# Six gate operations of each batch move from VectorE to GpSimd, and the listed order is laid out anew

## The chip, the cores and the metric

The kernel runs on one core of one Trainium2 chip, as one launch. The metric is device time in microseconds (us), the lower the better. Before the change the median of three runs was 641.9 us (641.13 to 643.39).

## The reference

The program computes an attention layer with a decay and feeds its result into a mixture of experts, each of which is an attention layer of its own. There are 8 batches, 8 heads, 576 positions, a head dimension of 64, 4 experts, and two experts are chosen for each position.

```python
# attention with decay, for each batch and head
scores = scale * np.matmul(q, k.transpose(0, 1, 3, 2))
log_f = np.log(np.clip(f, 0.0001, 1.0))
cum = np.cumsum(log_f, axis=-1)
decay = cum[:, :, :, None] - cum[:, :, None, :]
scores = np.where(causal, -1000000000.0, scores + decay)
scores = scores - np.max(scores, axis=-1, keepdims=True)
attn = np.exp(scores)
attn = attn / (np.sum(attn, axis=-1, keepdims=True) + 1e-09)
attn_out = np.matmul(attn, v)
# x = attn_out with the heads side by side: (batch, position, 512)
logits = x @ w_gate
topk = np.argpartition(-logits, K, axis=-1)[..., :K]          # K = 2
w = softmax of the two chosen logits
for e in range(E):                                            # 4 experts
    q, k, v = x @ wq[e], x @ wk[e], x @ wv[e]
    ye = causal_softmax(scale * q @ k.T) @ v @ wo[e]
    out += (e is chosen) * w * ye
```

## The kernel before, in words

**Units of work.** The kernel works on pairs: two heads of one batch (32 units of kind `a`), or two experts of one batch (16 units of kind `m`). Each unit goes through `max_pass` (the row maxima of the scores, found with one cheaper product), `scores` (the scores again, more exactly, as two products that accumulate in PSUM, then the exponential) and `attend` (the product with the values). Two units form a group, for which `row_sums` and `apply_rows` divide by the sums of the exponentials. For a batch's experts `moe_front` first makes the values and the gate logits (`pv`, line 439), then the gates; `prep_moe` makes queries and keys (`pp`, line 544); `project_out` multiplies by the output weights (`po`, line 936).

**Engines.** TensorE makes all products. VectorE takes the maxima out of PSUM with a masked reduction (line 624, with an accumulator that is read by a second instruction, and line 640), and makes the low parts of numbers that are split in two (lines 399, 557 and 913), the multiplication by the reciprocal sums (line 886) and small steps. ScalarE makes the exponentials (lines 734, 744, 750, 765) and copies out of PSUM. GpSimd cuts the causal diagonals out of the exponentials (line 703), and adds the exponentials of a unit up to a narrower tile, `R`, in four additions (lines 776, 778, 780, 782), whose columns TensorE then sums (line 839).

**The gates** (lines 469 to 525, in `moe_front`). With `lg` the logits of 128 positions by 5 blocks by 4 experts, `g4` and `t4` (128 by 80 numbers) hold for each pair of experts whether one is at least as large, and larger, than the other. `g4` is multiplied by an upper triangle (477), `t4` by a lower one (479), and the two are added (481), so that a tie goes to the lower number. `wins` counts and compares with 1.5 (484, 486). Then `mx` is the largest logit (489), `gt` the difference (492), its exponential on ScalarE (494), its product with `wins` (496), `sm` its sum, plus 1e-9, and the reciprocal (499, 501, 503), and `gt` times that (505). TensorE turns the gates with 16 small products (`pg`, line 512), VectorE copies them to `gc` (521, 525), and `row_sums` of the experts multiplies the reciprocal sums by `gc` (862).

**Order.** Each task (one of the functions above for one unit, group or batch) is a Python generator; each `yield` ends a step. `ORDER` is a text of 4939 steps: two characters name the task whose next step is issued. At the end every instruction is tied to the one before it on its engine, so each engine runs its own instructions in the order of this text, and the five engines and the DMA queue of SyncE (SP) meet only where one waits for another's data or buffer:

```python
    for x, y in zip(digits[::2], digits[1::2]):
        i = DIGITS.index(x) * len(DIGITS) + DIGITS.index(y)
        ...
        next(started[i], None)
    ...
        if ins.engine in behind:
            tc.add_manual_dep(ins, behind[ins.engine], order, reason="in order")
```

`SLOTS` lists in the same way which buffer each new tile takes: the 8 banks of PSUM, 20 strips, 5 wide tiles and so on. The 110 matrix products of `keep_warm` (`warm`, line 205) do no work for the result; 100 of them stand in the list before the first product of `scores`.

**The start and the end.** The first unit has a maximum pass of its own form (`max_by_head`, lines 566 to 606). The last tasks of the list are the `row_sums`, `apply_rows` and `project_out` of the last batch's experts.

Of the kernel before, what the change touches and what calls it, by code (L numbers as in the profile page):

```python
# [32 lines left out]
0e0e0e0e4z0e080303080h080e0e0e080808080h08080808080h08080h0e080e0e0j0j0j0o0t040e0j0j0j0e0e080808080808084w4w080e
0j0j0o0o0j0j0j0j0j0j0j0j0j0j0j0j0j0j0j0j0e0j0o0h0f0f0f0f0o0f0f0o0o0q0f09080j0t0j090f0f080f0f0f0f03080q0A0q0f0q0q
0q0j0j0q0f0f0f0f0q0q0t0q0k0k0k0A0q0k0q0d0f0f0q0k0t0k0k0k0a0t0t0k0a0a0a0a0f0q0F040k0k0k0q0k0q0k0f0k0q0q0f0k0q0i0k
0k0q0q4A0q0q0q0k0k0k0k0k0f0q0v0v0v0v0v0v0f0v0v0v0v0p0v0A0k0q0A0a0A0F0a0g0v0v0v0v0v0v4A0v0v0g0t0k0q0o0v0l0v0q0l0a
0q0q0B0t4y0a090C0C0v0v0v0v0v0C0g0C0C0C0C0C0C0C0C0r0r0r0r0r0r0r0r0b0f0r0r0r0r0r0C0C0C0r0v0v0v0v0C0C0C0r0r0r0r0C0C
0N0C0r0k0r0r0C0C0r0C0C0m0m0m0C0F0F0F0C0m0s0b0m0l4A0O0b0b0m0m0b0b0C0b0C0b0w0w0w0w0w0A0w0w0w0w0w0w0w0w0b0H0H0H0H0H
0H0H0m0m0w0H0N4A0C0C0n0n0H0s0s0N0H0H0n0w0M0w0w0w0w0w0M0n0R0R0n0R0n0n0n0w0w0H0H0H4A0n0R0M0w0w0N0H0H0H0n0H0H0H0H0H
0r0n0H0H0b0A0M0H0N0N0R0R0A0Y0N0N0N0N0u0M0N0N0N0N0N0N0N0N0N0N0N0N0N0N0N0N0N0N0N0N0N0N0N0O0N0D0M0D0R0D0D0O0O0O0D0N  # L40
0r0O0O0r0O0M0M0O0O0D0D0D0D0O0D0N0H0D0D0O0O0D0D0O0D0D0D0O0O0G0F0O0O0O0D0H0H0O0w0r0w0D0H0F0F0x0H0N0D0D0D0Y0x0O4y0y
0b0+0y0M4A0I0Y0Y0Y0Y0I0I0I0O0O0N0O0M0M0O0I0I0I0I0O0I0I0I0I0I0I0I0I0I0y0I0I0I0I0I0I0I0y0y0y0R0Y0O0O0O0O0R0R0R0R0R
# [40 lines left out]
322X31312X31302T2X2X2T2X2T2T2X2X2X322T30302T2X3132303032322T303030302T2T2T2B2T3032313230302C303030302T2C302T3232
2T2X2T3c312X3c2X302I302C2C302C31312N2O2C322T2N2I322O2T2T322X2I323e32323232322Y323c2Y2O32322Y2Y2Y2Y2T2T2T2Y2O2Y35
3c2Y2Y32324y3e323e352Y2Y2Y2Y2Y3e322Y2Y2O2O3e3e2Y2Y2Y2Y2Y2Y2Y32323c2C4y3235353c353535353535352Y353535352Y35353535
35353535353535353532353h2T3e3e353e3e35352O2N3e332O2U35353o352C2C303333332C30303e3e333e2U3c36363636363636362U2D36
# [957 lines left out]
```

## Time and profile before

| | |
|---|---|
| Median of three runs | 641.9 us (641.13 to 643.39) |
| The profiled execution's own time | 642.41 us |
| Its span, from the first to the last instruction | 640.7 us |
| TensorE (PE) busy | 627.2 us, 98% |
| VectorE (DVE) busy | 541.1 us, 84% |
| ScalarE (ACT) busy | 481.9 us, 75% |
| GpSimd (POOL) busy | 409.7 us, 64% |
| DMA queue of SP, share of 16 engines | 43.7% |

A busy TensorE is not a TensorE at its peak: the products are pipelined, their ends are modelled, and idle times under 150 ns count as busy. So the 2% that are left are stalls that can be told one by one, with the engine that ended each. An instruction of VectorE or GpSimd is shown from its start to its end, which holds whatever kept it from its data.

### The profile page before, as it was taken

To read this page: it belongs to the slowest core of one execution; us is meant where nothing else is said; L and a number is where in the kernel's file an instruction comes from. 1 tells how busy PE (TensorE), PEld (TensorE's weight loads), DVE (VectorE), ACT (ScalarE), POOL (GpSimd) and SP (SyncE) were. 2 spreads that over 40 slices of the span, in tenths; PEclk is the share of its full clock that TensorE was granted. 3 is DMA by queue.
4 is the path that set the end of the run, shared out by engine and by line. 5 is a ranking of instruction groups with operands and counts; after the bars stand their busy time and mean duration, and the time that the engine had idled before them with its cause. 6 is when DMAs were issued, how large, how long until landed. Compare 5 with 4: busy or idle time off the path is not lost.

```text
span 640.7 us, 15170 instructions
## 1 busy us (share of the span) xinstructions
PE 627.2 (98%) x5303; PEld 538.1 (84%) x5303; DVE 541.1 (84%) x1541; ACT 481.9 (75%) x1057; POOL 409.7 (64%) x519
## 2 busy tenths in 40 slices
PE   8899999999999999989999999999999999999997
PEld 6677889789888988869888898887987789879976
DVE  6889998898988988988998898889788987787572
ACT  7899887897778867867688877877667896566654
POOL 8999499638748585284569664655848647533740
PEclk9999999999999999999999999999999999999999
DMA  6556425533555355512552461552435433241425
GB/s 195 154 168 194 136 55 143 137 90 96 141 140 130 80 158 144 161 55 62 170 145 66 148 174 40 139 142 83 119 105 136 134 109 76 79 98 21 107 70 202
DMA packets 33531, 76.90 MB, mean 120 GB/s; under 512 B 4395, under 2 KB 4875, under 8 KB 33455
## 3 DMA queue, kind: packets, MB, share of 16 engines
q1 hardware_dynamic: 33455, 75.94, 43.7%
q8 instruction: 42, 0.69, 0.4%
q14 instruction: 34, 0.28, 0.1%
HBM read 32.86 MB, written 10.35 MB: 67 GB/s over the span
## 4 chain that ended last, share of the span: by engine, by line
PE 88%; DVE 6%; issue 2%; DMA 2%; ACT 1%; SPq 1%; POOL 0%; DVEq 0%; POOLq 0%
PE pp_m L544 16%; PE ob_a L801 10%; PE pv L439 7%; PE po L936 7%; PE s_a L716 7%; PE s_a L717 7%; PE m_a L618 6%; PE m_m L618 4%; PE ob_m L801 4%; PE oa_a L801 4%; PE s_m L716 4%; PE s_m L717 4%; PE sm_a L839 3%; PE warm L205 2%; PE oa_m L801 1%
## 5 line engine op out<-in xcount | busy, mean ns | idle before, releaser
L703 POOL TENSOR_SCALAR_AFFINE_SELECT P_a<-P_a 128x256 f32<-128x256 f32 x128 | 65.3, 527 | 112.7 <-ACT P_a L734 67.2
L716 PE MATMUL s_a<-ka_a 128*128 128x320 f32 (+4 forms) x384 | 104.2, 296 | 1.1 <-DVE mxs_a L624 0.9
L717 PE MATMUL s_a<-kq 128*128 128x320 f32 (+4 forms) x384 | 102.9, 294 | 0.0
L624 DVE CUSTOM_DVE_ANT_0 junk_a<-m_a,mask 128x192 bf16<-128x192 f32 (+2 forms) x186 | 86.8, 486 | 17.3 <-PE m_a L618 15.4
L618 PE MATMUL m_a<-kq 128*128 128x448 f32 (+3 forms) x372 | 80.7, 304 | 4.0 <-DVE mxs_a L624 3.1
L552 ACT ACTIVATE kq<-pp_m 64x288 fp32r<-64x288 f32 x128 | 51.9, 406 | 31.6 <-PE pp_m L544 30.1
L716 PEld LDWEIGHTS s_a<-ka_a 128*128 128x128 f32 (+1 forms) x384 | 69.2, 180 | 4.4 <-DVE mxs_a L624 1.6
L717 PEld LDWEIGHTS s_a<-kq 128*128 128x128 f32 (+1 forms) x384 | 68.6, 180 | 1.2
L557 DVE TENSOR_TENSOR ka_m<-pp_m,kq 64x288 fp32r<-64x288 f32 x128 | 58.2, 454 | 12.9 <-ACT kq L552 9.7
L801 PE MATMUL ob_a<-P_a,va 128*64 128x320 f32 (+1 forms) x512 | 67.5, 406 | 0.0
L776 POOL TENSOR_TENSOR R_a<-P_a 128x896 f32<-128x896 f32 x32 | 67.5, 2110 | 0.1
L618 PEld LDWEIGHTS m_a<-kq 128*128 128x128 f32 (+1 forms) x372 | 57.6, 180 | 9.7 <-DVE mxs_a L624 4.4
L703 POOL TENSOR_SCALAR_AFFINE_SELECT P_m<-P_m 128x256 f32<-128x256 f32 x64 | 33.7, 543 | 48.2 <-ACT P_m L734 31.0
L778 POOL TENSOR_TENSOR R_a<-R_a,P_a 128x640 f32<-128x640 f32 x32 | 55.3, 1731 | 1.8
L801 PEld LDWEIGHTS ob_a<-P_a,va 128*64 128x64 f32 x512 | 35.8, 137 | 24.0
L716 PE MATMUL s_m<-ka_m 128*128 128x192 f32 (+2 forms) x192 | 51.8, 295 | 0.0
L717 PE MATMUL s_m<-kq 128*128 128x192 f32 (+2 forms) x192 | 50.9, 294 | 0.0
L624 DVE CUSTOM_DVE_ANT_0 junk_m<-m_m,mask 128x192 bf16<-128x192 f32 (+2 forms) x96 | 44.9, 485 | 5.3 <-PE m_m L618 4.3
L399 DVE TENSOR_TENSOR ka_a<-xin_a,ka_a 64x1152 fp32r<-64x1152 f32 x32 | 47.9, 1497 | 0.7
L734 ACT ACTIVATE P_a<-s_a 128x512 f32<-128x512 f32 x64 | 36.8, 598 | 13.2 <-PE s_a L717 12.0
L399 DVE TENSOR_TENSOR ka_a<-xin_a,kq 64x1152 fp32r<-64x1152 f32 x29 | 42.5, 1465 | 0.8
L618 PE MATMUL m_m<-kq 128*128 128x320 f32 (+3 forms) x192 | 41.2, 298 | 0.0
(204 smaller groups left out, 2025.3 us busy)
## 6 DMA issues: line engine op xcount, KB each, us to landing
xin_a<-in_qk_dram SPq DMA_DIRECT2D x32, 576.0 KB
va<-in_v_dram SPq DMA_DIRECT2D x32, 320.0 KB
bt_a<-rr_a SPq DMA_DIRECT2D x32, 288.0 KB
ka_m<-kq SPq DMA_DIRECT2D x32, 288.0 KB
kq<-ka_a SPq DMA_DIRECT2D x30, 288.0 KB
out_dram<-outb SPq DMA_DIRECT2D x32, 256.0 KB
...
```

The lines of the kernel that those rows point to most:

```text
L399: eng.tensor_tensor(lo, x[at], hi.bitcast(F32), ALU.subtract)
L544: nc.tensor.matmul(pp[:, :HS], w[:, c, es], x[c][:, gs], start=(n == 0), stop=(n == 3 * KC - 1))
L552: nc.scalar.activation(hv[h], src[h], AF.Copy)
L557: nc.vector.tensor_tensor(lo[:, h, gs], src[h], hv[h].bitcast(F32), ALU.subtract)
L618: nc.tensor.matmul(dst, qB[0:K, h, i0 : i0 + dst.shape[0]], kB[0:K, h, j0:j1], start=True, stop=True)
L624: nc.vector.tensor_tensor_reduce(jk[:, :n], src, mask[:, MW - n :], 1.0, init, ALU.add, ALU.max, acc)
L703: return nc.gpsimd.affine_select(pv, pv, [[0, 2], [1, 128]], ALU.is_ge, 0.0, base=0, channel_multiplier=-1)
L716: nc.tensor.matmul(dst, kaf[:, c : c + m], qA[:, h, i0:i1], start=True, stop=False)
L717: nc.tensor.matmul(dst, kqf[0:K, c + h * S : c + h * S + m], qB[0:K, h, i0:i1], start=False, stop=True)
L776: g.tensor_tensor(r[:, :, 128:S], p[:, :, 320:768], p[:, :, 768:1216], ALU.add)
L778: g.tensor_tensor(r[:, :, 256:S], r[:, :, 256:S], p[:, :, 1216:1536], ALU.add)
L801: mm = nc.tensor.matmul(dst[64 * h : 64 * h + 64, c0 : c0 + rhs.shape[-1]], vs[h][0:kp, blk], rhs, start=first, stop=last,)
```

## The change

Six operations of the gates are issued on GpSimd and no longer on VectorE: the two products with the triangles and their addition, the subtraction of the largest logit, the product with `wins`, and the product with the reciprocal. The steps and their number stay what they were: the same 4939 steps stand in the new list, in another order, and the slots are dealt out anew. No other instruction is added or taken away. In the new list 107 of the 110 `warm` products stand before the first product of `scores`.

```diff
 ORDER = """
-4w4w4w4w4w4w4w4w4w4w4w4w4w4x4x4x4w4w4y4w4w00024w004w4w004x074y014x0005054A4A054w4w4w4w4w4w4w4w4w4w4w4w4w4w4w4w4w
-4w4w4w4w4w4w4w4w4w4w4w4w4w4w4w4w4w4w4w4w4w4w4w4w4w4w4w4w4w4w05024y4y4y4y4w4y4y4w4w4w4y4w4w4w4A4A4A4A4A4A4A4A4A4A
...
+4w4w4w4w4w4w4w4w4w4w4w4w4w4w4w4w4w4w4w4w4w4w4w4w4w4w4w4w4w4w4w4w4w4w4w4w4w4w4w4w4w4w4w4w4w4w4w4w4w4w4w4w4w4w4w4w
+4w4w4w4x4x4x4x00020507004x004y4y4y4y004y4y4y4y4A4A4A4A4x4A4A4A4A4A4w4w4w4w4w4w4w4A4w4w05054A4w4A4w024w4w4w4w4w4w
...
 SLOTS = """
-P 01201201201021021021012010210120120120102101201021
+P 01201201201021020120102101201021012012010012010120
...
         nc.vector.tensor_tensor(t4, la, lb, ALU.is_gt)
         yield
-        nc.vector.tensor_tensor(g4, g4, up.unsqueeze(1).to_broadcast([128, 5, E, E]), ALU.mult)
-        yield
-        nc.vector.tensor_tensor(t4, t4, low.unsqueeze(1).to_broadcast([128, 5, E, E]), ALU.mult)
-        yield
-        nc.vector.tensor_tensor(g4, g4, t4, ALU.add)
-        yield
+        nc.gpsimd.tensor_tensor(g4, g4, up.unsqueeze(1).to_broadcast([128, 5, E, E]), ALU.mult)
+        yield
+        nc.gpsimd.tensor_tensor(t4, t4, low.unsqueeze(1).to_broadcast([128, 5, E, E]), ALU.mult)
+        yield
+        nc.gpsimd.tensor_tensor(g4, g4, t4, ALU.add)
+        yield
...
         gt = work.tile([128, 5, E], F32, tag="gt", name=f"gt{b}")
-        nc.vector.tensor_tensor(gt, lg, mx.unsqueeze(2).to_broadcast([128, 5, E]), ALU.subtract)
+        nc.gpsimd.tensor_tensor(gt, lg, mx.unsqueeze(2).to_broadcast([128, 5, E]), ALU.subtract)
         yield
         nc.scalar.activation(gt, gt, AF.Exp)
         yield
-        nc.vector.tensor_tensor(gt, gt, wins, ALU.mult)
+        nc.gpsimd.tensor_tensor(gt, gt, wins, ALU.mult)
         yield
...
-        nc.vector.tensor_tensor(gt, gt, sm.unsqueeze(2).to_broadcast([128, 5, E]), ALU.mult)
+        nc.gpsimd.tensor_tensor(gt, gt, sm.unsqueeze(2).to_broadcast([128, 5, E]), ALU.mult)
         yield
```

## Rows read from the trace of the kernel before

**Rows 1.** The page: span, busy time by engine, TensorE in 40 slices

```profile
span 640.7 us, 15170 instructions
...
PE 627.2 (98%) x5303; PEld 538.1 (84%) x5303; DVE 541.1 (84%) x1541; ACT 481.9 (75%) x1057; POOL 409.7 (64%) x519
...
PE   8899999999999999989999999999999999999997
```

**Rows 2.** Busy time by stretch: length, then PE, PEld, DVE, ACT, POOL

```profile
0.00:48.00 48.00, 41.71 (x308) 33.21 (x309) 38.55 (x106) 40.27 (x62) 45.09 (x56) 1.00 0.56 172
48.00:273.00 225.00, 225.00 (x1935) 193.89 (x1935) 202.97 (x583) 181.35 (x399) 151.83 (x197) 1.00 0.49 129
273.00:284.00 11.00, 8.65 (x71) 6.58 (x65) 9.89 (x20) 7.61 (x17) 9.87 (x10) 1.00 0.22 60
284.00:429.00 145.00, 145.00 (x1275) 126.29 (x1274) 127.10 (x375) 109.36 (x243) 88.14 (x113) 1.00 0.43 115
429.00:437.00 8.00, 7.60 (x60) 5.99 (x58) 7.31 (x15) 7.18 (x16) 7.80 (x11) 1.00 0.72 208
437.00:622.00 185.00, 184.21 (x1599) 160.09 (x1601) 149.67 (x436) 126.86 (x303) 106.95 (x137) 1.00 0.35 92
622.00:640.70 18.70, 15.03 (x73) 12.10 (x69) 5.63 (x12) 9.24 (x21) 0.00 (x0) 0.99 0.57 186
```

**Rows 3.** Waits of TensorE's products: us in total, times, longest

```profile
PE m_a L618 <- DVE mxs_a L624: 3.1, 4, 1.1
...
PE mp_a L685 <- DVE mxs_a L624: 1.3, 2, 0.7
...
PE s_a L716 <- DVE mxs_a L624: 0.9, 1, 0.9
```

**Rows 4.** VectorE in order of time, 273 to 284 us and at 430: start, duration

```profile
274.57 2.54 DVE L913 TENSOR_TENSOR xl_a<-ot_a,xh_a 128x576 fp32r<-128x576 f32 x1
...
280.53 2.15 DVE L913 TENSOR_TENSOR xl_a<-ot_a,xh_a 128x576 fp32r<-128x576 f32 x1
...
430.15 3.83 DVE L886 TENSOR_TENSOR ot_a<-bt_a,ot_a 128x576 f32<-128x576 f32 x2 [0.47 <-DMA bt_a<-rr_a]
```

**Rows 5.** GpSimd in order of time, 273 to 284 us

```profile
274.39 2.10 POOL L776 TENSOR_TENSOR R_m<-P_m 128x896 f32<-128x896 f32 x1
...
279.96 2.11 POOL L776 TENSOR_TENSOR R_m<-P_m 128x896 f32<-128x896 f32 x1
```

**Rows 6.** TensorE's products in order of time, 273 to 284 us

```profile
280.66 0.39 PE L618 MATMUL m_a<-kq 128*128 128x256 f32 x1 [1.06 <-DVE mxs_a L624]
...
283.42 1.03 PE L618 MATMUL m_a<-kq 128*128 128x448 f32 x6 [1.14 <-DVE mxs_a L624]
```

**Rows 7.** Groups by line, the six operations: busy us, mean ns, idle before

```profile
L505 DVE TENSOR_TENSOR gt<-gt,sm 128x20 f32<-128x20 f32 x8 | 3.2, 398 | 0.2
...
L496 DVE TENSOR_TENSOR gt<-gt,wins 128x20 f32<-128x20 f32 x8 | 2.7, 333 | 0.8 <-ACT gt L494 0.8
...
L492 DVE TENSOR_TENSOR gt<-vm,mx 128x20 f32<-128x20 f32 x8 | 2.3, 287 | 0.2
...
L481 DVE TENSOR_TENSOR g<-g,t 128x80 f32<-128x80 f32 x8 | 2.2, 274 | 0.2
...
L477 DVE TENSOR_TENSOR g<-g,up 128x80 f32<-128x80 f32 x8 | 2.0, 247 | 0.0
...
L479 DVE TENSOR_TENSOR t<-t,low 128x80 f32<-128x80 f32 x8 | 1.8, 225 | 0.0
```

**Rows 8.** Lines 913, 782 and 614: duration ns, min/median/max, first and last start

```profile
L913 DVE TENSOR_TENSOR xl_a<-ot_a,xh_a x32: 694/754/2540, 67.3 to 576.1; 128x576 fp32r<-128x576 f32 x32
...
L782 POOL TENSOR_TENSOR R_a<-R_a,pl x32: 447/454/1652, 47.3 to 563.5; 64x128 f32<-64x128 f32 x32
...
L614 POOL MEMSET mxs_a<- x31: 92/95/102, 5.4 to 527.1; 64x2 f32 x31
```

**Rows 9.** Chain that ended last, its end: start, duration

```profile
622.53 14.52 PE po L936 x63
```

More of the change, by code (lines that the diff above doesn't have):

```diff
@@ L33 @@
[L33 to L42, printed above, removed]
@@ L83 @@
[L83 to L86, printed above, removed]
-2O3e333333333e3333362D362D35333333332T36353636363636363e3e3e3333362W36332D333333333336303e3e3e3e3h3h3h36363e3636
@@ new lines @@
+4w4w4w4w4w4w4w4w4w054A0505004A4A00004w0005020202020202020202020c4w4w4w4w4w4w024y4y4y4z024w4w4w014w02020602020202
+0702020707024w4w074z0c074w024w4w4w4w4w4w4w0202020202024w0c000c07020202070707070c050c0303070c07070707070707074w07
+0h4w03030303034z4z4z07070303030303030e0e0e07030303070e0e0e0303030e4w0307074z4z4z07030e0303070d0e0e0j0e0e0e0e0h0e
+0e0e0h0504040c070c0h0h040e0e0e0808030308080808080h0h0e0e0e08080808080e0e08080e080j0j0j0j0j0j080e08030e080o0j0j0j
+0j08080j0j0o0j0t08080j0o0j0j080j0j0j0j0q0j0j0j0j0j0h0e0e0f0f0f0f0f0f0f0f0f0f0f08080f0o0o0o0o0j090j0f0t0f0f0f0f08
@@ new lines @@
+090q0q0q0f0q0q0q0q0q0q0j0j0t0k0f0k0k0k0k0k0k0k0f0f0A0q0t0t0k0k0k0k0k0t0i0q0q0q0q0q0q0q0q0q0q0q0q0f0a0f0a0a0k0k0k
+0k0k0p0v0k0q0v0k0q0v0a0v0v0f0v0k0A4A0F0A0a0A0a0v0v090v0v0g0k0g0v0f0a0k0v4A0g0v0v0v0v0v0v0v0v0v0v0q0v0q0A0k0q0q0o
+0q0k0k0t0l0a0C0C0C0t0l0F0v0f0v0a0v0C0C0C0C0C0C0C0l0r0r0r0r0r0r0r0r0r0r0r0r0v0C0v0r0b0C0b0r0C0v0C0r0C0C0C0C0r0C0v
+0r0r0C0C0m0F4A0r0w0m0r0r0r0m0m0m0b0m0b0w0w0w0w0w0w0w0w0F0C0F0m0b0b0w0b0b0w0w0w0C0C0s0m0A0C0b0m0s0w0s4A0H0H0H0H0H
+0w0w0w0H0w0H0n0H4y0H0n0n4A0M0N0N0N0w0H0R0R0R0n0n0n0n0n0H0w0M0M0n0n0N0R0w0H0H0C0H0H0H0H0H0H0H0C0M0H0A0H0N0N0M0N0N
@@ new lines @@
+0N0N0N0N0C0R0w0H0O0N0N0N0N0w0C0N0N0C0w0A0N0N0N0N0N0N0N0N0N0N0N0N0N0N0N0N0M0N0H0D0D0M0M0Y0M0u0H0O0O0O0O0B0H0r0r0D
+0D0H0O0M0H0D0D0O0w0O0M0D0w0D0O0r0O0D0D0D0D0D0r0D0D0D0D0H0O0O0F0O0O0O0O0O0O0O0O0H0D0D0D0D0R0F0F0O0O0x0y0y0n0y0y0y
+0Y0Y0M0N0O0O0I0I0I4A0G0I0I0I0I0I0O0I0I0I0I0N0I0N0I0I0I0I0I0x4A0Y0Y0Y0O0O0O0I0O0I0I0Y0R0R0R0S0R0b0M0R0R0R0R0R0R0R
+0R0R0R0R0R0R0R0+0x0D0+0+0+0+0+0I4y0R0R0R0+0R0R0R0R0D0P0b0R0R0R0+0+0+0M0M0I0y0+0S0S0S0S0M0M0M0S0S0S0S0P0I0I0P0S0S
+0M0M0O0P0P0y0P0M0+0S0S0S0S0S0P0P0P0P0P0P0P0S0+0P0R0D0M0S0M0S0D0D0P0+0P0P0S0S0S0P0P0P0P0P0S180S0S0S0+0+0Y0+0+0+0+
@@ new lines @@
+0+0+0R0+110I0y0R0z0M180M0R0M0M0M0M0M0M0M0y0P0+0S0S0S0M0S0P0J0E110K110E0+0z0+0+0+0T0K0M0M0J0M0P0J0E0M0T0T0T0T0T0T
+0T0M0z0z0T0T0T130K0P1111111313131313131313131f110T0+0+130T0T0T0T0T0T0T180T0T0Q0-18180K0K0Q0M0T0T1313130Z0M131313
+0K13130-1d0-0Q0-13131313130M0T0-120-0-0-0-0-130-0-0-0-0-0-0-0K0-0-13130K0K1a1a1a0M0z0z0z0z1a1a1a1a1a1a1a0T1a0M0M
+0-0-0-131813110L0M1d1d0M180U0U10100U130L1a141a0L141a141a1a1414141414141414141k14141d1d0T0L14141014190L0z0L0L1a1a
+1a1a0z0L1l1l1a1a1a1a1a1l0L1f1a141414140V0M1a1e0V0V1l0-141a1a0M0M1f181a1f1f1f1l1l1f1l1f1l1w0V1f0V0V1l1l1p1l1f1l1l
@@ new lines @@
+1l1b1l1l1b1l1b1b1l1l1l1l1l1l1b1b1b1k1k1k1k1k1b1b1f1f1d0-0V0V1b1b1f1f1f1f1f1f1f1f1f0-4A4A1b4A4A0V1l1l1l1l1l1l1l1l
+1l1p1f1b1b1k1k1k1k1b1l1l1f1f1m1f1p1d1d1b141k1b0z1f1m1b14141l1l141f1f1p1p1p1p1f0W1p1p0-1m1p1p1p1m1m1m1b1b1b1b1m1f
+1p1m1m1b1p1p1p1p1p1p1p1l1l1b0W0L1q1p1p1p1p1p1p1p1p1p1p1p1p1p1p1q161b1q1q1q161w160L1q1g1g1g1g1g1g1q1q161g1q1q1B16
+1g1g1g1g161m1k1q0V1m161g1k1k1k1g1g1g1g1g1g1g1g1g160W1b1m1m1m1m1g1g1k1k1g1g1k0W1q1q1q1q1m1m1m1g1m1m1m1m1m1q1q1q1m
+1q1w1q1q1q1q1w171B1m1c1m171w151h1w0W1h151m1k1m1m1y1y1p1m1k1p151w0W0W1y1p0W1y1k1k1k1k1y1y1y1y0W1y1c1c1I1k1k1k1n1n
@@ new lines @@
+1k1n1k1k1q1q1n1n1n1n1n1y1n1n1n1p1q1n1q1k1k1k1n1n1n1q1y1n1n1n1D1i1i171i1i1q1q4A1h1y1y1y1y1y1y1y1y1y1y1y0X1n1n1n1B
+1I1n1n1k1k171r1B1B17161r1r1r1r1r1r1r1r1r1r1r1r1C1r1r1r1y1B1n1y1r1r1N1n1y1y1B1r1r1r1o1o1o1I1I1I1B1y1D1i1D1D1D1D1r
+1r1r1D1D1D0X0X1D1r1y0X0X0X1D1x1D1D1D1i1D1D1D1y1D1D1D1s1s1n171D171y0X171k1i1s1D1w0X1D1i1i1J1N1K1K1K1K1K1K1K1K1K1K
+1D0X0X1D1D1z1z1K1r1z1z1z1z1z1z1z1K171k1K0X1z1K1K1K1K1k1k1k1k1z1K1z1K1K1K1D1D0X1D1D1z1z1z1j1k1k0X0X1k1K1j1z1z1z0X
+1j1k1k1t1k1t1U1K1K1z1N1N1N1V1V1k1k1z1j1j1j1j1V1V1j1j1E1N1E1E1E1E1E1E1U1U1E1K1K1E1E1E241E1E1P1t1U1E1E1E1E1E1E1E1E
@@ new lines @@
+1E1I1I1K1K1V1V1V1V1V1V1Z1P1P1Z1K1V1P1P1P1P1P1P1P1P1V1V1K1E1I1U1V1V1V1W1z1V1Z1Z1Z1L1L1L1L1L1L1Z1U1N1U1U1U1Z1t1L1V
+1P1P1P1L1L1L1L1L1L1L1L1L1L1t1L1Z1t1P1z1P1P1t1t171P171V1V1V1V1V1V1V1V1t1t1L1U1U291z1z1P1V1Z1V1V1V1V0W1Z1W1z1z1P1P
+1V1L1Z1Z1Z1V1W1V1V1V1L0W1V1V1W1W1W1Z1Z1E1E1W1W1W1W1N1E1P1P1P1P1P4y1Z1Z1Z1L1L1Z1Z1Z1Z1Z1Z1Z1Z1Z1Z1Z1Z1Z1Z1P1P1u1G
+1Z1Z1u2g1L1u1u1u1G1F1P1P1L1L1A1A1+1Q1F1F1Q1Q1W1+1Z1Z1+1Z1+1U1+1G1Q1+1+1+1+1A1Q1Q1G1Q1Q1Q1Q1Q1Q1+1Q1G1W1+1W1W1Q1Q
+1W1u1W1W1j1W1W1Q1Q1Q1W1Q1j1W1W1Q1Q1W1W1+1+1+1+1+1Q1Q1G29241W1U1U1U1U1U1U1U1Z1U241O1+1Q1Q1Q1W1G1G1G241U1+1+1+1+1+
@@ new lines @@
+241+1W1W1u1+1+1M1M1M241R1S241u1H1S1S1S1u1u1u1+1S1W1H1H1+1H1+1U1U1U1U1U1U1W1U1U1U1U1U1X1X1X1X1R1R2626261X1X1X1H1H
+1H1v1v1+1X26261v1v1+1U1U26261X2626261S1S1S1U1v1X1X1X1X1X1X261v1X1X1-1X261X2626261X2929291S1X1X1U2626261-1-1-1-1-
+26262626261X1-1-1H26262625291v1v1v1T1-1-1-1v2b1-2a1-1-1-1v1v1v1v1-1-1v291H1v2b1-1-1-261-1v1v2b2b2b2b1v2b2b2b2b1-
+2626261-1-1-1Y2b1U2g2g24202g2b201U1Y1U1T201U1T1T2l1T1T1T2b2b27271U2b2b2b272b2b272b1T1U1U1T1Y272727271U1U1X272b2b
+2s2727272727272i2g2i2i2i2i2i2i2i27272i2i2i2s2s2s2s2s292b2s2b2b2s1v2s2i1-1X2i2i2i2i2b2i2i2i1U2i272i1X2l212i212121
@@ new lines @@
+2g211U2b1U1U2i272b2b2b212s2s2s2s2s2s2s2s2s274y2l212l2s272n2t2t2t2c2c2c2t1H2c2c2c2c2c2c2c2c2c2c2l2l2l2c2c2c4y2i27
+2i2t2i21211H2c2c2c2c2c2c2727272g2t2t2i2t2t2t2t2t2t2t2t2t2t2t2t2t2t2t2c2i2i2i2g2l2n2t2n2n2n2n2n2n2n2t2x2n2t2n2s2s
+2s2s2s2s2s2t2t2t2t2t2t1T2c2n2s2n2n2t2t2c2n2n2n2n1T2n2c2u2t2t2t2j2t2u2n2n2n2j222u2u2u2n2n2s2s2s2n2s2s2s2s2j2u2221
+222822222d222d2n2n2d2u222u282u2j2u2E222s2u2s222n2j2j2j2j2j2j2j2j2n2n272j2j2j2u2s2u2j2j2h282u2u2u2u2u2u2u2u2j2E2u
+2E2u2E2e2e2o2o2o2j2m2j2e2j2j2u2u2x2x2o2o2o2o2o2o2o2o2o2x2x2x2o2o2o2o2o2o2o2o2o2s2x2u2t2e2E2E2Q2e2y2o2o2o2E2o2u2j
@@ new lines @@
+2u2u2x2x2x2x2x2x2x2x2x2x2x2x2x2x2x2x2x2x2x2x2x2x2x2x2x2x2x2x2s2x2x2x2u2e2e2e2J2y2k2y2G2G2y2y2y2y2y2y2G2G2E2y2G2y
+2v2p2p2p2f2k2o2y2y2y2y2v2v2j2f2j2y2y2y2y2v2s2j2y2y2y2v2G2v2v2v2v2v2v2v2v2y2y2f2G2v2s2G2G2y2v2v2G2v2v2v2v2v2G2y2e
+2q2k2q2J2y2v2v2v2G2v2G2G2G2G2G2G2G2G2G2G2G2G2y2G2y2y2G2w2J1v2G2Q2G2s2z2z2z2z2f2z2z2z2z2z2f2z2z2L2w2s2J2J2J232z23
+2f2q2z2f2z2z2z2z2J2v2G2L2z2V232z2z2q2z2q2z2L2L2z2z2z2z2G2L2L2L2L2L2L2L2s2s2q2Q2H2H2323232q2q2q2L2L232L2L2L2L2s2L
+232L232H2J2Q232H232L2H2H2H2H2L2L2L2S2L2Q2f2L2H2H2H2H2H2H2H2H2H2H2H2L2L2L2L2L2H2w2H2r312f2B2s2B2B2A2r2s2s2A2r2r2r
@@ L116 @@
+4i4i4u3L4i4u4u4u4u3L4u3L3L3L3L3L3L3L3L3L4u4u4u4u4u3L3L4j4j4j4j4j4j4j4j4j4j3L3L4j4j4j4j4j4j4v4i4v4v4v4v4v4v4v4v4v
 4v4v4v4v4v4v4v4v4v4v4v
```

117 lines of the change are left out of this document (41 added, 76 removed).

## The prediction

> **What bounds the kernel now.** I read the page first. TensorE is busy for 627.2 of 640.7 us; VectorE comes next with 541.1, and GpSimd has 640.7 - 409.7 = 231 us without work [rows 1]. So the end is set by TensorE, and only its 13.5 us of idle time can be won as long as the products themselves stay what they are; the change touches none of them. Second I asked for busy time by stretch, cut where the 40 slices show less than nine tenths, to see in which stage these 13.5 us lie [rows 2]. The start, up to 48 us, holds 48.00 - 41.71 = 6.3; the end, from 622 us, holds 18.70 - 15.03 = 3.7, which is the way of the last outputs behind the last product; between them lie only 2.35 at 273 to 284, 0.40 at 429 to 437 and 0.79 just behind it, 3.5 together. From 48 to 273 and from 284 to 429 us TensorE has no gap that the profile shows. Third, the waits by engine: what ends the gaps of TensorE is nearly always a maximum that VectorE still owes. The three rows make 3.1 + 1.3 + 0.9 = 5.3 us, those of the start included [rows 3].
>
> Fourth, the two long gaps in order of time, because they show the mechanism on which I build. TensorE stood for 1.06 and for 1.14 us before a product of the maximum pass, which waited for a PSUM bank that VectorE had not yet read [rows 6]. VectorE was late because a subtraction of two tiles in SBUF took 2.54 and 2.15 us [rows 4], while the same instruction has a median of 754 ns and a minimum of 694 [rows 8]. Both began 0.2 and 0.6 us after one of GpSimd's long additions had begun (274.39 for 2.10 us, 279.96 for 2.11 us), and both ended 0.6 us after its end, about what they take alone [rows 4, 5]. The gaps from 429 us on have the same mark ahead of them: two multiplications of two tiles in SBUF took 3.83 us together [rows 4]. So a VectorE instruction with two inputs in SBUF can lose 1.4 to 1.8 us beside an addition on GpSimd, and everything behind it on VectorE's queue is late by as much. This is what the middle of the run still loses.
>
> The Trainium skill names the same thing (GPSIMD Engine Reference, section Specifications): GpSimd's interface to SBUF is shared with VectorE, with contention when a VectorE instruction has two SBUF inputs. By that rule the trace agrees, with 2540 ns against 694 for one instruction [rows 8], and it speaks against a change that puts more two-input work on GpSimd; what it would do here is the third rival.
>
> **The change, part by part.**
>
> *VectorE loses six operations a batch.* Eight of each kind took 3.2 + 2.7 + 2.3 + 2.2 + 2.0 + 1.8 = 14.2 us in all [rows 7], 1.8 us a batch. Nothing of it is on TensorE's path by itself: VectorE has 640.7 - 541.1 = 99.6 us of slack [rows 1]. It counts only where VectorE is late for TensorE, and after the start that is the 3.5 us above. The price on the path is between 0 and -3.5 us.
>
> *GpSimd gets 48 small operations.* The trace of before has none of this size there. From below: a memset that reads nothing takes 95 ns, 48 x 0.095 = 4.6 us. From above: the smallest addition, 64 partitions by 128 numbers, takes 454 ns at the median, 48 x 0.454 = 21.8 us. Ours have 20 or 80 numbers on 128 partitions and two inputs, so they are nearest to the addition; I take 0.4 us each, 19 us in all [rows 8]. The cover is GpSimd's 231 us without work [rows 1]. Where that cover is missing, in a stretch full of additions such as 273 to 284 us, where GpSimd is busy for 9.87 of 11.00 [rows 2], one operation makes the cuts and additions behind it late by its 0.4 us, and at the worst by the 1.65 us that the longest of these small additions took [rows 8].
>
> *New waits.* The six are no longer neighbours on one engine. GpSimd waits for VectorE's comparisons, for the largest logit, for ScalarE's exponential and for the reciprocal; VectorE waits for GpSimd before it counts the wins and before it sums. Behind a waiting operation on GpSimd stand the diagonal cuts, for which `attend` waits, and the additions of `R`, for which the `sm` products wait. At the end TensorE waits for the last product before its 16 `pg` products. I counted in the two lists how many TensorE instructions stand between the last gate operation and `pg`: for batches 0 to 7 the old list has 16, 15, 10, 130, 51, 36, 19 and 36, the new one 77, 8, 53, 52, 21, 57, 90 and none. So seven batches are covered about as before or better, and the last is not. There the new list puts the last three operations on GpSimd behind the last addition of `R`, with nothing else left in its queue. The chain from that addition is three operations of 0.4, and an exponential and three steps of VectorE at 0.225, the shortest of the small ones [rows 7]: 3 x 0.4 + 4 x 0.225 = 2.1 us. Beside it runs the `sm` step, which needs the same addition, and the new list has all three remaining `attend` steps ahead of `sm`, where the old one had two. I therefore cost it at 0, with 0 and +2.1 as ends.
>
> *The list.* All steps are issued in another order, the SP queue's transfers too: values, gate weights and the rows of extra terms at the start stand in another order there, and each waits for what is ahead of it. I compared the two lists by counts. At the start they do the same in nearly the same order: 107 instead of 100 warm products ahead of the first scores, and one more reduction of VectorE ahead of the last maximum of the first unit. TensorE's 6.3 us of idle time there [rows 2] are bounded by -6.3 and by +2.3, two gaps as long as the longest of rows 6; I take 0. At the end the old list has 30 output products of batches 5 and 6 behind the last `attend` and before the first of batch 7; the new one has 48, but none of the `attend` work. The last stretch of products is dense in the old run, 63 in 14.52 us [rows 9], and I see nothing in the new list that would open it: 0, with -0.5 and +1 as ends.
>
> *What decides* is then which of VectorE's two-input instructions meet an addition on GpSimd. The old run has three such meetings that reach TensorE in the middle, worth 3.5 us. They are accidents of that list and its drift; the new list puts other instructions side by side. Six operations fewer a batch leave fewer candidates on VectorE and more room behind each of them, while 48 short operations are added on the other side. I take half a meeting as left, 0.5 us (between none and one of 1.1).
>
> **Sum.** From the profiled execution's own 642.41 us: -3.5 for the meetings of the old list, +0.5 for those of the new one, 0 for GpSimd's 19 us, 0 for `pg`, the start and the end. That is 639.4 for such an execution. It stands 0.5 us above the median of the three runs, so the forecast is 638.9 us; its own range is 637.5 to 641.
>
> **The rivals.**
>
> *The relief does not reach TensorE.* For it: in 555 of the 640 us TensorE idles for no more than 0.8 [rows 2]. Then the new list has as many meetings as the old one: 641.9 us. Against it: two of the six operations are themselves two-input instructions that were stretched, since 398 and 333 ns for 20 numbers is more than the 247 ns for 80 [rows 7].
>
> *More is won at the start.* The same 6.3 us of idle time lose half, by luck of the new order, and the middle loses all its gaps: 641.9 - 3.5 - 3.1 = 635.3 us. For it speaks that VectorE's maxima end most of these waits too; against it that the gates begin long after.
>
> *The list meets more additions* (the slower side). The place is `apply_rows` and the splits of line 399 beside the additions of `R`, which the 48 new operations push later than the list expects. Each meeting that reaches TensorE costs 1.1 us [rows 6]. With seven where three were, the time is 641.9 + 4 x 1.1 = 646.3 us; it gets slower from the fourth meeting on. For it: GpSimd's stretches beside additions are already full [rows 2]; against it: each new operation holds the interface for 0.4 us and not for 2.1.
>
> *`pg` waits.* The chain of the last batch is laid bare with 2.1 us, or GpSimd's queue makes the gates of several batches late, while the gaps of the middle stay: 641.9 + 2.1 = 644.0 us.
>
> **How the numbers follow.** The forecast gets 0.38, the unreached relief 0.17, the better start 0.15, the meetings 0.23, `pg` 0.07. A difference under 0.3%, 1.9 us, can't be told from none in this kernel, so faster means below 640.0 and slower above 643.8. Of the forecast's 0.38 some 0.30 lies below 640.0. Faster: 0.30 + 0.15 = 0.45; same: 0.08 + 0.17 = 0.25; slower: 0.23 + 0.07 = 0.30. The range for 8 in 10 goes from 633.5, below the better start by a further part of the 6.3 us, to 647.5, one meeting above the slower case.
>
> **What would show it.** In the profile after, VectorE should be busy for about 527 us and GpSimd for about 429. The two-input subtraction of line 913 should show fewer than two durations above 2 us in front of a gap of TensorE, and TensorE's waits for VectorE after 48 us should be about 0.5 us. The six operations should take about 0.4 us each on GpSimd. Wrong would be: gaps of TensorE over 3 us in the middle, a wait of `pg` for GpSimd, or a start whose idle time is no longer near 6.3 us; in these cases the layout and not the move has decided.

## The result, and the profile after

The change makes the kernel slower by about 1%: 650.25 us median of three runs (648.23 to 650.49) against 641.9, ratio 1.0111 (95% interval 1.0091 to 1.0132). A ratio here is estimated from all runs; it is not the quotient of the two medians. The profiled execution took 650.25 us, its span 648.5. The forecast of 638.9 us has the wrong sign, and its range ended at 647.5.

The page of the changed kernel answers to [rows 1]:

```profile
span 648.5 us, 15130 instructions
...
PE 628.2 (97%) x5303; PEld 540.4 (83%) x5303; DVE 546.3 (84%) x1493; ACT 481.1 (74%) x1057; POOL 429.4 (66%) x567
...
PE   8898999999999999999999999979999899999997
...
PEclk9999999999999999999999999998999999999999
```

TensorE's idle time is now 648.5 - 628.2 = 20.3 us, where it was 13.5: 6.8 more. Its busy time is 1.0 more. Together that is the 7.8 us by which the span grew. GpSimd has the 429 us that were forecast. VectorE lost 14.2 us of work and is busy for 5.2 us *more*: what stayed on it takes 19.4 us longer.

Busy time by stretch, columns as in [rows 2]:

```profile
0.00:48.00 48.00, 41.81 (x313) 34.17 (x314) 39.74 (x106) 41.02 (x66) 45.63 (x56) 1.00 0.57 174
48.00:273.00 225.00, 220.18 (x1889) 189.48 (x1888) 202.73 (x558) 173.94 (x385) 159.47 (x208) 1.00 0.45 120
273.00:430.00 157.00, 157.00 (x1376) 135.87 (x1375) 136.72 (x390) 121.65 (x271) 105.33 (x141) 1.00 0.48 125
430.00:440.00 10.00, 6.66 (x41) 5.01 (x41) 8.78 (x15) 5.24 (x9) 6.85 (x8) 0.89 0.35 89
440.00:622.00 182.00, 179.76 (x1532) 158.05 (x1530) 147.81 (x399) 125.99 (x301) 109.71 (x151) 1.00 0.36 90
622.00:648.50 26.50, 22.83 (x166) 17.80 (x162) 10.50 (x28) 13.25 (x30) 2.40 (x6) 1.00 0.55 174
```

Start (6.2) and end (3.7) are what they were. The stretch from 273 us, which held 2.35 us of gaps before, has none. But 48 to 273 lost 4.8 us, 430 to 440 lost 3.3 and 440 to 622 lost 2.2: the middle went from 3.5 to 10.4 us. TensorE's waits, as in [rows 3], name VectorE, not GpSimd and not `pg`:

```profile
PE oa_m L801 <- DVE mxs_a L624: 4.8, 2, 3.3
PE m_a L618 <- DVE mxs_a L624: 3.5, 3, 1.8
...
PE s_m L716 <- DVE mxs_a L624: 1.4, 1, 1.4
PE pp_m L544 <- DVE xl_a L913: 1.3, 1, 1.3
```

Ahead of each long gap stands a VectorE instruction that took much longer than it does alone, as in [rows 4 to 6]; I call it held. The longest gap, in order of time (start, duration):

```profile
430.88 5.29 DVE L886 TENSOR_TENSOR ot_a<-bt_a,ot_a 128x576 f32<-128x576 f32 x2
...
431.45 2.10 POOL L776 TENSOR_TENSOR R_m<-P_m 128x896 f32<-128x896 f32 x1
...
433.63 1.93 POOL L778 TENSOR_TENSOR R_m<-R_m,P_m 128x640 f32<-128x640 f32 x1
...
436.10 0.61 DVE L624 CUSTOM_DVE_ANT_0 junk_a<-m_a,mask 128x448 bf16<-128x448 f32 x1
...
436.86 0.87 PE L801 MATMUL oa_m<-P_m,vm 128*64 128x256 f32 x8 [3.35 <-DVE mxs_a L624]
```

Two multiplications that take 0.75 us each alone took 5.29 together. The maximum behind them on VectorE's queue was late, and the bank that `attend` wanted came free with it. The first and the third long gap have an instruction ahead of them that the prediction did not count as a candidate, the addition of 1e-9 to 128 by 18 sums (the median of line 857 is 0.18 us):

```profile
50.44 2.11 POOL L776 TENSOR_TENSOR R_a<-P_a 128x896 f32<-128x896 f32 x1
...
51.80 0.45 DVE L624 CUSTOM_DVE_ANT_0 junk_a<-m_a,mask 128x320 bf16<-128x320 f32 x1
52.19 2.66 DVE L857 TENSOR_SCALAR rc_a<-zt_a 128x18 f32<-128x18 f32 x1
...
52.47 0.12 POOL L614 MEMSET mxs_a<- 64x2 f32 x1
...
52.53 0.78 POOL L703 TENSOR_SCALAR_AFFINE_SELECT P_a<-P_a 128x256 f32<-128x256 f32 x2
...
53.26 1.55 POOL L778 TENSOR_TENSOR R_a<-R_a,P_a 128x640 f32<-128x640 f32 x1
...
56.77 1.02 PE L618 MATMUL m_a<-kq 128*128 128x256 f32 x6 [1.82 <-DVE mxs_a L624]
```

```profile
191.87 2.50 DVE L857 TENSOR_SCALAR rc_a<-zt_a 128x18 f32<-128x18 f32 x1
191.92 2.10 POOL L776 TENSOR_TENSOR R_m<-P_m 128x896 f32<-128x896 f32 x1
193.99 0.34 POOL L479 TENSOR_TENSOR t<-t,low 128x80 f32<-128x80 f32 x1
...
194.82 0.39 PE L716 MATMUL s_m<-ka_m 128*128 128x256 f32 x1 [1.39 <-DVE mxs_a L624]
```

The maximum of line 624, which reads PSUM, ran beside GpSimd's first addition in its usual 0.45 us; VectorE's small addition was held until 54.85, through a memset, two cuts of the diagonal and the second addition. At 191.87 it ended at 194.37, when the moved gate operation of line 479 ended too. The other gaps stand behind line 913, which took 2.42 us (gap of 1.28 at 147), and line 399, which took 2.74 (gap of 0.62 at 506) and 3.40:

```profile
509.58 3.40 DVE L399 TENSOR_TENSOR ka_a<-xin_a,ka_a 64x1152 fp32r<-64x1152 f32 x1
509.66 2.11 POOL L776 TENSOR_TENSOR R_m<-P_m 128x896 f32<-128x896 f32 x1
...
515.38 0.87 PE L801 MATMUL oa_m<-P_m,vm 128*64 128x256 f32 x8 [1.45 <-DVE mxs_a L624]
```

1.82 + 1.28 + 1.39 + 3.35 + 0.62 + 1.45 = 9.9 of the 10.4 us. The six moved operations answer to [rows 7] (busy us, mean ns, idle before); three of them:

```profile
L477 POOL TENSOR_TENSOR g<-g,up 128x80 f32<-128x80 f32 x8 | 4.6, 569 | 3.5 <-DVE g L473 3.5
L505 POOL TENSOR_TENSOR gt<-gt,sm 128x20 f32<-128x20 f32 x8 | 4.0, 502 | 2.5 <-DVE sm L503 2.5
...
L496 POOL TENSOR_TENSOR gt<-gt,wins 128x20 f32<-128x20 f32 x8 | 1.8, 228 | 7.0 <-ACT gt L494 7.0
```

All six take 17.8 us, and GpSimd waits 17.2 us for their inputs.

### The profile page after: what moved, and what is told of

It reads as the page before. It is cut to its first block, busy times and chain, and to the rows that moved or that the text cites. A ratio compares the mean times of both kernels' runs of the same rounds, so it can differ in the third digit from the quotient of the medians.

```text
span 648.5 us, 15130 instructions
## 1 busy us (share of the span) xinstructions
PE 628.2 (97%) x5303; PEld 540.4 (83%) x5303; DVE 546.3 (84%) x1493; ACT 481.1 (74%) x1057; POOL 429.4 (66%) x567
## 4 chain that ended last, share of the span: by engine, by line
PE 84%; DVE 7%; ACT 3%; DMA 2%; issue 2%; POOL 1%; SPq 0%; DVEq 0%; POOLq 0%; ACTq 0%
PE pp_m L544 16%; PE ob_a L801 9%; PE pv L439 7%; PE s_a L717 7%; PE s_a L716 7%; PE po L936 6%; PE m_a L618 6%; PE ob_m L801 5%; PE m_m L618 4%; PE oa_a L801 3%; PE s_m L716 3%; PE s_m L717 3%; PE sm_a L839 3%; DVE junk_a L624 2%; DVE ka_a L399 2%
## 5 line engine op out<-in xcount | busy, mean ns | idle before, releaser
L703 POOL TENSOR_SCALAR_AFFINE_SELECT P_a<-P_a 128x256 f32<-128x256 f32 x128 | 72.1, 580 | 106.0 <-ACT P_a L734 70.5
L624 DVE CUSTOM_DVE_ANT_0 junk_a<-m_a,mask 128x448 bf16<-128x448 f32 (+2 forms) x186 | 86.5, 484 | 13.8 <-PE m_a L618 10.7
L618 PE MATMUL m_a<-kq 128*128 128x448 f32 (+3 forms) x372 | 78.3, 302 | 4.2 <-DVE mxs_a L624 3.5
L703 POOL TENSOR_SCALAR_AFFINE_SELECT P_m<-P_m 128x256 f32<-128x256 f32 x64 | 30.8, 495 | 43.9 <-ACT P_m L734 28.9
L778 POOL TENSOR_TENSOR R_a<-R_a,P_a 128x640 f32<-128x640 f32 x32 | 53.4, 1667 | 1.7
L716 PE MATMUL s_m<-ka_m 128*128 128x256 f32 (+3 forms) x192 | 52.1, 296 | 1.4 <-DVE mxs_a L624 1.4
L624 DVE CUSTOM_DVE_ANT_0 junk_m<-m_m,mask 128x320 bf16<-128x320 f32 (+2 forms) x96 | 44.8, 485 | 8.0 <-PE m_m L618 7.4
L717 PE MATMUL s_m<-kq 128*128 128x256 f32 (+3 forms) x192 | 50.8, 294 | 0.0
L399 DVE TENSOR_TENSOR ka_a<-xin_a,kq 64x1152 fp32r<-64x1152 f32 x29 | 46.1, 1588 | 0.8
L618 PE MATMUL m_m<-kq 128*128 128x320 f32 (+4 forms) x192 | 41.8, 299 | 0.0
```

The costliest lines, as they stand in the source:

```text
L399: eng.tensor_tensor(lo, x[at], hi.bitcast(F32), ALU.subtract)
L618: nc.tensor.matmul(dst, qB[0:K, h, i0 : i0 + dst.shape[0]], kB[0:K, h, j0:j1], start=True, stop=True)
L624: nc.vector.tensor_tensor_reduce(jk[:, :n], src, mask[:, MW - n :], 1.0, init, ALU.add, ALU.max, acc)
L703: return nc.gpsimd.affine_select(pv, pv, [[0, 2], [1, 128]], ALU.is_ge, 0.0, base=0, channel_multiplier=-1)
L716: nc.tensor.matmul(dst, kaf[:, c : c + m], qA[:, h, i0:i1], start=True, stop=False)
L717: nc.tensor.matmul(dst, kqf[0:K, c + h * S : c + h * S + m], qB[0:K, h, i0:i1], start=False, stop=True)
```

## The experiments

Medians, ratio to the kernel before measured beside it (its medians there are 642.3 to 643.7, single runs 640.2 to 649.7), and TensorE's idle time (span less busy, from each page). The kernel before idles for 13.5, the changed one for 20.3. Where a run adds lines, its line numbers run on: L890 of e9 is line 886, L778 of e3 and e9 the first addition of line 776.

| run | median us | ratio, 95% interval | idle us |
|---|---|---|---|
| e1_newlist_dve | 662.75 | 1.0278 (1.0232 to 1.0324) | 27.9 |
| e2_oldlist_pool | 662.27 | 1.0275 (1.0229 to 1.0320) | 26.6 |
| e3_newlist_split | 695.80 | 1.0787 (1.0734 to 1.0840) | 47.1 |
| e4_oldlist_split | 721.35 | 1.1184 (1.1136 to 1.1233) | 65.1 |
| e5_new_no857 | 645.51 | 1.0027 (0.9999 to 1.0055) | 14.2 |
| e6_new_move886 | 649.15 | 1.0072 (1.0040 to 1.0103) | 17.8 |
| e7_new_chain | 647.28 | 1.0042 (1.0014 to 1.0070) | 17.2 |
| e8_old_chain | 651.52 | 1.0108 (1.0054 to 1.0162) | 19.9 |
| e9_new_wait1 | 645.43 | 1.0030 (1.0000 to 1.0059) | 16.6 |
| e10_new_waits_no857 | 647.49 | 1.0055 (1.0021 to 1.0090) | 17.2 |
| e11_old_waits | 649.73 | 1.0114 (1.0077 to 1.0151) | 19.1 |
| e12_old_no857 | 643.86 | 1.0007 (0.9969 to 1.0046) | 13.9 |
| e13_new_no857_wait1 | 639.31 | 0.9908 (0.9871 to 0.9944) | 11.9 |
| e14_old_pool_but_last | 653.61 | 1.0162 (1.0118 to 1.0205) | 20.5 |
| e15_new_four_waits | 639.42 | 0.9925 (0.9898 to 0.9952) | 12.2 |

**The layout or the move?** e1 takes the changed kernel, e2 the kernel before, and each swaps the engine of the six operations alone:

```diff
-        nc.gpsimd.tensor_tensor(g4, g4, up..., ALU.mult)     # e1: all six; e2: the reverse
+        nc.vector.tensor_tensor(g4, g4, up..., ALU.mult)
```

> The new list and its slots, with the six gate operations back on VectorE. If the layout decides (where the list puts VectorE's two-input work beside the additions of R), the time stays near that of the changed kernel, 648 to 652 us, with about 10 us of idle time of TensorE in the middle. If the move decides (48 waits and 17.8 us more on GpSimd), it falls back to 641 to 644 us with about 3.5 us idle in the middle.

> The old list and its slots, with only the six gate operations moved to GpSimd. If the layout decides, 640.5 to 643.5 us: the old meetings stay where they were, and VectorE is relieved of up to 14 us of which at most 3.5 count. If the move decides, 648 to 652 us. A third theory, that any change of the timing throws the meetings anew whatever the list, would make both this one and the new list with the old engines slower than 643.5.

Both main theories fail: each mixture is some 12 us slower than the changed kernel. The third theory of e2, that any change of timing makes new meetings, came out as it said; e12 below speaks against "any".

e1 shows something more. Five of the six long gaps stand in it too, behind the same instructions, although none of the six operations has moved: 1.81, 1.03, 3.34, 0.62 and 1.44 us, together 8.2. So these gaps come with the new list and not with the move. The longest, in e1:

```profile
436.92 5.29 DVE L886 TENSOR_TENSOR ot_a<-bt_a,ot_a 128x576 f32<-128x576 f32 x2
...
442.90 1.51 PE L801 MATMUL oa_m<-P_m,vm 128*64 128x256 f32 x7 [3.34 <-DVE mxs_a L624]
```

Back on VectorE, the six operations are held beside additions as well: lines 505 and 477 have means of 806 and 593 ns, where [rows 7] have 398 and 247 (single ones make these means: the longest of line 505 took 3.46 us, the median is 0.18). In e2 GpSimd waits 45 us for inputs of the gates (17.2 in the changed kernel), and at the end TensorE waits for it:

```profile
PE sm_m L839 <- POOL R_m L782: 7.6, 1, 7.6
```

In order of time, GpSimd in e2, with the row that shows the wait in its queue:

```profile
620.82 0.37 POOL L477 TENSOR_TENSOR g<-g,up 128x80 f32<-128x80 f32 x1 [5.76 <-DVE g L473]
621.16 2.11 POOL L776 TENSOR_TENSOR R_m<-P_m 128x896 f32<-128x896 f32 x1
...
631.64 0.22 POOL L505 TENSOR_TENSOR gt<-gt,sm 128x20 f32<-128x20 f32 x1 [1.70 <-DVE sm L503]
631.82 2.07 POOL L776 TENSOR_TENSOR R_m<-P_m 128x896 f32<-128x896 f32 x1
```

e14 tests that row by giving the last batch's six back to VectorE (`gate = nc.vector if b == B - 1 else nc.gpsimd`, old list):

> The old list with the six operations on GpSimd in batches 0 to 6 and on VectorE in the last batch. With all eight on GpSimd it took 662 us, and one gap of 7.59 us at 629 stands behind the last additions of R, which GpSimd makes only after operations of the last gates that wait for VectorE. If these waits in GpSimd's queue are the price of the move at the end, that gap goes and the time is 653 to 655.5. If the end is late for another reason, it stays at 660 to 663.

The gap at the end is gone, 653.61 us. So the move costs the old list 19 us, nearly 9 of them in GpSimd's queue at the end. The other 10 are not followed up here; in e14 TensorE waits 6.6 us for maxima (3.1 before) and 2.0 for a diagonal cut of GpSimd. The new list takes the wait at the end away (it has the last three operations behind the last addition), and no wait of TensorE there names GpSimd.

**Shorter additions.** e3 and e4 cut the three long additions into independent quarters, e7 and e8 into halves by head that wait for one another:

```diff
-        g.tensor_tensor(r[:, :, 128:S], p[:, :, 320:768], p[:, :, 768:1216], ALU.add)
+        for h in range(2):                     # e3, e4; the second and third addition likewise
+            for o in range(0, 448, 224):
+                g.tensor_tensor(r[:, h, 128+o : 352+o], p[:, h, 320+o : 544+o], p[:, h, 768+o : 992+o], ALU.add)
...
+        a1(0), a2(0); yield; a3(0), a1(1); yield; a2(1), a3(1); yield      # e7, e8
```

> The changed kernel with each of the three long additions of R cut into four pieces that give the same sums (12 instructions a unit where there were 3; GpSimd's busy time rises). If VectorE's instructions are held until the addition beside them ends, they are now held for one piece of about 0.6 us, not for up to 2.1: durations of lines 913, 886, 399 and 857 above 2 us go, the idle time of TensorE in the middle falls from 10.4 to 3 to 5 us, and the time to 643 to 646 us. If VectorE is held for the whole row of pieces, or if the gaps come from elsewhere (a wait for GpSimd's results), it stays at 649 to 655 us.

> The kernel before with the same cut of the three long additions. If held VectorE instructions are what TensorE loses in the middle, its 3.5 us fall to 1 to 2 and the time to 639 to 641 us. If the longer busy time of GpSimd delays the sums instead, it rises to 643 to 648 us.

Both came out far above the times written for them, 695.80 and 721.35 us. Here my first picture, that an instruction is held for one of GpSimd's, fell. e3 in order of time:

```profile
178.08 2.54 POOL L778 TENSOR_TENSOR R_a<-P_a 128x224 f32<-128x224 f32 x4
...
179.16 6.02 DVE L399 TENSOR_TENSOR ka_a<-xin_a,ka_a 64x1152 fp32r<-64x1152 f32 x1
180.57 2.00 POOL L782 TENSOR_TENSOR R_a<-R_a,P_a 128x160 f32<-128x160 f32 x4
182.52 1.45 POOL L786 TENSOR_TENSOR R_a<-R_a,P_a 128x96 f32<-128x96 f32 x4
184.05 1.86 POOL L788 TENSOR_TENSOR R_a<-R_a,pl 64x128 f32<-64x128 f32 x2
```

Twelve pieces follow one another without a pause, and VectorE, which began beside the second of them, is held through all the rest. It gets in at the first pause, 0.08 us at 183.97, ahead of an addition that waits for the piece before it; then that addition is the one that is held. Of the 30 instructions that lost over 0.8 us in e3 against their median, each was held across the ends of 3 to 11 GpSimd instructions. 21 of them got in within 0.25 us of a pause in GpSimd's row, which was 0.08 us long for 15 of them and longer for 6; what let the other 9 in, the trace does not show. The uncut additions wait for each other, so they have such pauses; the pieces took them away. e7 and e8 put them back:

> The changed kernel with the three long additions of R cut into halves by head, in the order first, second, third of one head and then of the other, so that nearly every piece waits for the one before it (6 pieces of 0.5 to 1.1 us). The traces of the cut into independent pieces show VectorE held through a whole row of pieces that follow without a gap, and let in where a piece waits for the one before it (a gap of 0.08 us). If that is the rule, VectorE is now held for at most about 1.1 us or so, and the time falls to 643 to 648. If VectorE is held until GpSimd's queue is empty, or if the price is that of any change of the durations, it rises to 655 to 700 as with the independent pieces.

> The kernel before with the same additions in dependent halves. By the rule of gaps its longest held instructions fall from 1.8 to 2.3 us of excess to about 1, and the time is 639 to 643. If any change of GpSimd's durations throws the meetings anew, 645 to 665.

In e7 no long gap behind the start names VectorE any more (line 399 takes at most 2.60 us, was 4.27), but GpSimd is busy for 464.6 us and `R` is late for `sm` seven times:

```profile
PE sm_a L852 <- POOL R_a L795: 3.6, 5, 1.0
...
PE sm_m L852 <- POOL R_m L795: 1.5, 2, 1.3
```

In e8 that price is larger than what the old list had to win: 651.52 us falls in the second branch, with `sm` waiting where VectorE no longer does.

**Taking one held instruction away.** e5 (and e12, in the old list) leaves out line 857:

```diff
-        nc.vector.tensor_scalar(rc, zt[:, :, 0], 1.0e-9, None, ALU.add)
         yield
-        nc.vector.reciprocal(rc, rc)
+        nc.vector.reciprocal(rc, zt[:, :, 0])
```

> The changed kernel without the step of line 857 (1e-9 added to sums that are about 1 or more; the reciprocal reads the sums directly). It leaves that addition out. Two gaps of TensorE, 1.82 us near 55 and 1.39 near 193, stand behind two of these small instructions of 128x18 that took 2.66 and 2.50 us instead of 0.18. If being held beside GpSimd is what makes these gaps, both go and the time falls by about 3 us to 646 to 648; if the maxima are late for another reason (or the next small instruction is held in the same way), the gaps stay and the time is 649 to 651.

> The kernel before without the step of line 857 (1e-9 added to the sums is left out). None of its 24 instructions was held there (0.17 to 0.36 us), so by the theory nothing of TensorE's 3.4 us in the middle goes: 640 to 643.5 us, no change. If taking out small VectorE work helps or throws the meetings by itself, the time moves by more than 2 us either way.

In e5 both gaps are gone, and the time falls by 4.7 us, more than the 3.2 they held: the gaps of lines 913 and 399 at 147 and 515 vanished as well, without a cause that I can name (in e13 the first is back). In the old list, where none of the 24 was held, no change shows (ratio 0.9969 to 1.0046). So it is the meeting and not the work.

e6 moves the two multiplications of line 886 and the two copies behind them past five VectorE instructions of the next maximum pass:

> The changed kernel with four entries of the list put eight to fourteen places later, near 430 us: the two multiplications of line 886 and the two copies behind them now come after five maxima of the next unit. If the held multiplications (3.29 and 2.08 us) make the gap of 3.35 us there, the gap falls below 1 us, the granted clock of 0.89 behind it goes, and the time falls by 3 to 4 us to 646 to 647.5. If that stage is late for another reason, the gap stays or only moves: 649 to 651.

The gap only moved and shrank to 2.46 us, against the expectation. The multiplications still took 3.31 us, now beside lines 776 and 778, the copies on ScalarE waited 4.45 us for them, and now the exponentials behind the copies were late:

```profile
430.67 3.31 DVE L886 TENSOR_TENSOR ot_a<-bt_a,ot_a 128x576 f32<-128x576 f32 x2
...
437.12 1.16 PE L618 MATMUL m_a<-kq 128*128 128x192 f32 x5 [2.46 <-ACT P_a L734]
```

e9 leaves the list as it is and lets GpSimd's addition wait for the multiplications at this one place:

```diff
+        if nm == "_m4_1":
+            together(first, two_inputs["last"])     # GpSimd waits for the second of line 886
```

> The changed kernel with one wait more: at one place (expert unit 1 of batch 4, near 431 us) GpSimd's first long addition waits for the two multiplications of line 886 that the list has ahead of it. If the multiplications are late because the addition runs beside them, they take about 0.8 us each, the gap of 3.35 us near 433 falls below 1 us, the rest of the trace stays as it is, and the time falls by 2.5 to 3.5 us to 646.5 to 648. If the addition is not the cause, the gap stays at about 3.3 us and the time at 649 to 651.

```profile
431.17 1.68 DVE L890 TENSOR_TENSOR ot_a<-bt_a,ot_a 128x576 f32<-128x576 f32 x2
...
433.00 2.10 POOL L778 TENSOR_TENSOR R_m<-P_m 128x896 f32<-128x896 f32 x1 [0.72 <-DVE ot_a L890]
```

1.68 us instead of 5.29, the gap of 3.35 gone, 645.43 us. GpSimd gave 0.72 us. The same wait everywhere is too much of it:

> The changed kernel without the step of line 857 (1e-9 added to the sums is left out), and with each of the 48 first additions waiting for the last two-input instruction of VectorE (lines 399, 886, 913) that the list has ahead of it. Without line 857 alone it took 645.5 us, with 4.4 us idle in the middle, 3.35 of it in one gap. If the waits only turn the order round where both are ready, the middle falls to 1 to 2 us and the time to 641 to 643. If they make R late, waits of the sm products for GpSimd appear and the time is 646 to 660.

> The kernel before with the same 48 waits. Its three meetings in the middle are of lines 913 and 886 beside a first addition; if the list has them ahead of the addition, they go and the time falls to 638 to 641. If R becomes late, sm waits and the time is 644 to 655.

Both missed the hoped-for branch. In e11 `R` comes late by 6.1 us in one wait of `sm_m`; in e10 GpSimd is late for TensorE three times, by 1.8, 1.1 and 0.8 us, and a maximum pass waits 2.5 us for ScalarE. With the two single repairs together (e5 and e9):

> The two single repairs of the changed kernel together: without the step of line 857 (1e-9 added to the sums is left out) and with the one wait of GpSimd's addition near 431 us. Without line 857 alone TensorE idled for 4.4 us in the middle, 3.35 of it in the gap that the wait took away by itself. If the gaps are separate and each is one held instruction, about 1.0 us is left in the middle and the time is 640.5 to 642, at or just below the kernel before. If taking one away lets another in, it is 643 to 647.

It came out better than expected: 639.31 us. The last run leaves nothing out and adds four waits, one at each of four gaps:

```diff
+        if nm == "_m1_0": together(first, late[857, "_a2_2"])
+        if nm == "_a2_0": together(first, late[913, "_a1_2", 1])
+        if nm == "_m4_1": together(first, late[886, "_a5_2", 0])
+        if nm == "_a0_2": together(second, late[857, "_a0_0"])
```

> The changed kernel, nothing left out, with four waits of GpSimd for VectorE: its first addition in unit 0 of batch 2's heads waits for the subtraction of line 913 before it, that of expert unit 0 of batch 1 for line 857, that of expert unit 1 of batch 4 for line 886, and its second addition in unit 2 of batch 0's heads for line 857. These are the four gaps of 1.28, 1.39, 3.35 and 1.82 us. If each is made by GpSimd's addition alone, they fall to 0, 0, 0 and about 0.5; the middle falls from 10.3 to 2.5 to 3.5 us, the clock of 0.89 behind the longest goes, and the time is 640.5 to 643. If a held VectorE instruction is only late for something else, or GpSimd's additions become late for TensorE, the time stays above 645.

639.42 us, 0.9925 of the kernel before (0.9898 to 0.9952): this version beats both kernels with all of the arithmetic. Its page, and the two longest of TensorE's waits behind the start:

```profile
span 637.1 us, 15132 instructions
...
PE 624.9 (98%) x5303; PEld 538.9 (85%) x5303; DVE 536.8 (84%) x1493; ACT 481.1 (76%) x1057; POOL 429.1 (67%) x567
```

```profile
PE oa_m L811 <- DVE mxs_a L626: 1.4, 1, 1.4
...
PE m_a L620 <- DVE mx_a L675: 0.6, 1, 0.6
```

All four gaps are gone; these two are the ones of line 399 that no wait was given to. Against the changed kernel the span is 11.4 us shorter, 8.1 of it idle time. The other 3.3 are busy time of TensorE. Up to 1.7 of them can be the clock, which was granted at 0.66 of full speed for the 5 us from 437 to 442 of the changed kernel; the rest is not settled.

## Why the prediction was wrong

*What bounds the kernel* held: TensorE, and its gaps in the middle.

*VectorE loses 14.2 us, GpSimd gets 19*: the sizes held (17.8 measured). `pg`, the start and the end at 0 held too: 6.2 and 3.7 us, and no wait for GpSimd.

*-3.5 for the meetings of the old list*: right for the two gaps between 273 and 284 us, which are gone. The third place, near 430 us, became the longest gap of all.

*+0.5 for the meetings of the new list*: this is the step that failed. It measured 9.9 us in six gaps. Three things were wrong in it. First, "six operations fewer leave fewer candidates" does not follow: the instructions that reach TensorE are those of lines 857, 886, 399 and 913, and all of them stayed. Second, the candidates were taken to be two-input instructions alone; two of the six gaps stand behind line 857, with one input. The Trainium skill states it (SBUF — State Buffer, section Who interferes with whom): a `tensor_scalar` can take the port pair that VectorE shares with GpSimd, the first to issue has it for its whole instruction, and the loser blocks. The trace agrees that the small addition is held, 2.66 and 2.50 us against 0.18; it does not agree that this lasts for one instruction, since the first of the two was held through several of GpSimd's. I had weighed only the rule on two inputs. Third, a meeting was priced at 1.1 us. e3 shows that it does not end with the addition, but mostly at a pause in GpSimd's row of instructions. One pair of multiplications cost 3.35 us, and then the clock.

*The list meets more additions*, the third rival, names the mechanism and three of its four lines (886, 913 and 399, not 857), and gave 646.3: seven meetings were assumed, six gaps of 0.6 to 3.35 us were found. Its reason, that the 48 operations push the additions later, is not shown for the new list. At 191.87 a moved operation lengthens the row that holds VectorE by 0.3 us, no more, and five of the six gaps are there without the move (e1). In the old list (e2) they do push them: TensorE waits up to 7.6 us for an addition.

*"The layout and not the move has decided"*: for the gaps of the changed kernel that holds, since 8.2 of their 9.9 us come with the new list alone (e1). But either half of the change by itself costs 19 us or more, so the move is not free either. That each list fits the engines it was laid out for would explain this; it is not shown.
